# The second head mix of a talking-heads kernel, from two fp16 parts to float32 quarter tiles

## The chip, the core and the metric

One NeuronCore of a Trainium2 chip runs the whole program. Its engines run beside each other, each with its own instruction stream: TensorE (PE in the rows; PEld is its weight loads), VectorE (DVE), ScalarE (ACT), GpSimd (POOL) and SyncE (SP), which here issues the DMA transfers. The metric is the device time of one execution in microseconds (us), as the median over runs.

## The reference, cut to what matters

Talking-heads attention, then a gated MLP (only its attention part is touched by the change):

```
scores = q @ k^T / 8                          # 4 batches, 12 heads, 448 x 448, head size 64
scores = einsum('bhij,hg->bgij', scores, w_pre)    # first mix over the heads
p      = exp(scores - max over j);  p = p / (sum over j + 1e-9)
attn   = einsum('bhij,hg->bgij', p, w_post)        # second mix over the heads
x      = attn @ v                             # heads joined to 768 columns
out    = x + (gelu(x @ w_in)[u] * (w_sg @ layernorm(gelu(x @ w_in)[v]) + b_sg)) @ w_out
```

All data is float32 (w_in, w_out: float64).

## The kernel before

**Groups.** The rows of a score matrix (448 per batch) are cut into groups of 10 queries, 45 per batch and 180 in all. A group is a tile of 128 partitions: in each half of 64 stand 5 queries x 12 heads = 60 rows (and 4 that hold nothing), with the 448 keys along the free dimension. Such a tile makes both mixes a matmul over partitions: the first mix (`premix`, L962) contracts 60 rows with a block-diagonal w_pre, and so does the second (`postmix`, L1037) with w_post.

**A group's way** is the generator `slot` (L1080): row maximum on VectorE (L993), exp with its row sum on ScalarE (L1000, writes the float32 tile `p32`), the reciprocal of the sum, `rs` (L1005, L1006); then one of three preparations of the second mix, then `postmix` on TensorE, then `evict` (L1133), which copies the product from PSUM to `at16`, from where `av` (L1160, L1185) multiplies with v.

**The three preparations before.** Groups 9 to 44 are *full*: `w_norm` (L1008) multiplies a [128, 120] table of w_post by `rs`, and `postmix` runs four float32 matmuls on the whole 128x128 array (L1044: 112 key columns of p as stationary weights, 120 moving columns). All others make fp16 parts: either `p_hi_of` and `p_lo_of` (L1018, L1023: high part of p times rs, then the rest), or `p_norm`, `p_hi`, `p_lo` (L1028, L1013, L1032: normalise in place, high part, rest). Their `postmix` runs 24 fp16 matmuls as two row tiles of 64x128 (L1056: 3 products of parts x 4 key blocks x 2 halves, 60 moving columns). Two such groups, a pair, go through TensorE in one burst.

**TensorE's other work.** `qk_mm` (L842, L849) makes the scores of a pair of heads with 64x128 row tiles (chunks of 64 queries: 64x64 quarter tiles); `premix` uses 64x64 quarter tiles; `av` 128x64 column tiles; the MLP (`products`, L1210, L1217, and L1430) mostly the whole array. A tile mode is how the 128x128 array is divided; it changes whenever two neighbours in TensorE's order use different modes.

**The order** is set when the program is built: `Plan.run` (L294) takes the next step of each stream by due ranks and planned costs (pairs are due by their group number; steps that several engines can do go to the one that is planned to end first) and writes every engine's instructions in that order. An engine then runs its list strictly in order and waits where data is late. `mode_of` (L221) tells the planner the tile mode; a change of it costs a step C_MODE in the plan. Score parts go through DRAM (`s_d`): written by `write` (L872), fetched back as groups by `load_pair` (L939).

**Buffers.** `p32` has 3 buffers (N_P32), each freed when the fp16 parts are made (full groups: when `postmix` has run); the fp16 parts have rings of 4. The fp16 `postmix` of every pair uses the same two PSUM banks (`at2`), so it comes after the evictions of the pair ahead.

Of the kernel before, what the change touches and what calls it, by code (L numbers as in the profile page):

```python
# [10 lines left out]
F32 = mybir.dt.float32  # L11
F16 = mybir.dt.float16
# [3 lines left out]
ALU = mybir.AluOpType  # L16
# [20 lines left out]
N_P32 = 3  # L37
# [37 lines left out]
P_F32 = 0
P_ONE = (0, 1, .5, .5)
C_ONE = 1e9
D_ONE = 20
# [11 lines left out]
N_W = 0  # L90
# [9 lines left out]
def talking_heads_gmlp(ctx, tc, q, k, v, w_pre, w_post, w_in, g_ln, w_sg, b_sg, w_out, out):  # L100
    nc = tc.nc
# [51 lines left out]
    wpp = ctx.enter_context(tc.tile_pool(name="wpp", bufs=2))  # L153
# [30 lines left out]
    wpost = const.tile([P, H * NT], F32, name="wpost")  # L184
# [3 lines left out]
    wpc_hi = const.tile([P, H * NH], F16, name="wpc_hi")  # L188
    wpc_lo = const.tile([P, H * NH], F16, name="wpc_lo")
    p_ring = [[const.tile([P, (NC - 1) * TC + P], F16, name=f"p{w}{i}") for i in range(PR)] for w in "hl"]  # L190
# [8 lines left out]
    wpc32 = vn_hi.rearrange("p c f -> p (c f)")[:, 384:504].bitcast(F32)  # L199
# [21 lines left out]
    def mode_of(gen):  # L221

        name = gen.__name__
        if name == "slot":
            return "128x128" if gen.gi_frame.f_locals.get("full") else "64x128"
        if name == "all_parts":
            return "64x32"
        if name == "all_qk" and heads(gen.gi_frame.f_locals["i"]) == 4:
            return "64x64"
        return {"all_qk": "64x128", "all_premix": "64x64", "all_av": "128x64"}.get(name, "128x128")  # L230
# [782 lines left out]
    def p_hi(n):  # L1013
        x = st[n]
        x["ph"] = p_ring[0][n % PR][:, :S]
        cast(x["ph"], x["p32"])

    def p_hi_of(n):  # L1018
        x = st[n]
        x["ph"] = p_ring[0][n % PR][:, :S]  # L1020
        cast(x["ph"], x["p32"], x["rs"])

    def p_lo_of(n):  # L1023
        x = st[n]
        x["pl"] = p_ring[1][n % PR][:, :S]
        nc.vector.scalar_tensor_tensor(out=x["pl"], in0=x["p32"], scalar=x["rs"], in1=x["ph"], op0=ALU.mult, op1=ALU.subtract)  # L1026

    def p_norm(n):  # L1028
        x = st[n]
        cast(x["p32"], x["p32"], x["rs"])  # L1030

    def p_lo(n):  # L1032
        x = st[n]
        x["pl"] = p_ring[1][n % PR][:, :S]
        diff(x["pl"], x["p32"], x["ph"])

    def postmix(n):  # L1037
        x = st[n]
        w = H * NT
        if "wp" in x:  # L1040
            ps = x["at"] = at_banks(False)[n % 2]
            at["next"] = n + 1
            for jc in range(NC):
                nc.tensor.matmul(ps[:TC, jc * w:(jc + 1) * w], lhsT=x["p32"][:, jc * TC:(jc + 1) * TC], rhs=x["wp"], start=True, stop=True)  # L1044
            return

        hi, lo = (r[n % PR] for r in p_ring)
        at2 = at_banks(True)
        w = H * NH
        o = x["col"]  # L1050
        for jc in range(NC):
            js = slice(jc * TC, jc * TC + P)
            for k, (l, r) in enumerate(((hi, wpc_hi), (hi, wpc_lo), (lo, wpc_hi))):
                for hf in range(2):
                    rows = slice(64 * hf, 64 * hf + 64)
                    nc.tensor.matmul(at2[:, hf, o + jc * w:o + (jc + 1) * w], lhsT=l[rows, js], rhs=r[rows],  # L1056
                                     start=(k == 0), stop=(k == 2))

    def at_views(n):
# [18 lines left out]
    W_NORM = {"act": 330, "dve": 192, "pool": 486}, {"act": 197, "dve": 192}  # L1078

    def slot(n, t):  # L1080
        b, c, _ = glist[n]
        i = NCH * b + ORD.index(c)
        t = yield "dve", 552, n - 3, t
        softmax_max(n)
        t = yield "act", 645, n - 2.5, t, lambda: after([past("exp", n - 1), past("p32", n - N_P32)])
        softmax_exp(n)
        tm["exp", n] = t
        t = yield "dve", 278, n - 2, t, lambda: past("r", n - 1)
        norm_r(n)
        tm["r", n] = t  # L1090
        full = ND <= n < N_F32 and (n < N_FULL or n * P_F32 % 1 < P_F32 or ck["pe"] < max(ck["dve"], ck["pool"]) + C_F32)
        if full:
            t = yield None, W_NORM[n < N_W], n - 1, t, lambda: after([past("ph", n - 1), past("post", n - 2)])
            w_norm(n)
            tm["pn", n] = tm["ph", n] = tm["pl", n] = t
        elif n * P_ONE[b] % 1 < P_ONE[b] or n >= D_ONE and ck["dve"] + C_ONE < ck["pool"]:
            t = yield None, {"act": 560, "dve": Shared(363), "pool": 640}, n - 1.5, t, lambda: after([past("ph", n - 1), past("post", n - PR)])
            p_hi_of(n)
            tm["pn", n] = tm["ph", n] = t
            t = yield "dve", Shared(600), n - 1, t, lambda: past("pl", n - 1)  # L1100
            p_lo_of(n)
            tm["pl", n] = tm["p32", n] = t
        else:
            t = yield None, dict(ones(S), act=590, dve=Shared(363), pool=620), n - 1.9, t, lambda: past("pn", n - 1)
            p_norm(n)
            tm["pn", n] = t
            t = yield None, ones(S), n - 1.5, t, lambda: after([past("ph", n - 1), past("post", n - PR)])
            p_hi(n)
            tm["ph", n] = t
            t = yield None, twos(S), n - 1, t, lambda: past("pl", n - 1)  # L1110
            p_lo(n)
            tm["pl", n] = t
            tm["p32", n] = t
# [368 lines left out]
    with tc.manual_schedule():  # L1482
        nc.vector.memset(neg_half, -0.5)
        nc.vector.memset(wpre32, 0.0)
        for r in p_ring:
            for x in r:
                nc.gpsimd.memset(x[:, S:], 0.0)
# [97 lines left out]
        def mix_weights(e):  # L1585
# [9 lines left out]
            e.tensor_tensor(  # L1595
                out=wpost.rearrange("p (g t) -> p g t", t=NT),
                in0=wrep[:, 1, :].unsqueeze(2).to_broadcast([P, H, NT]),
                in1=msk[:, 0:2, :].rearrange("p a b -> p (a b)").unsqueeze(1).to_broadcast([P, H, NT]), op=ALU.mult)
# [4 lines left out]
            e.tensor_copy(out=wpc_hi, in_=wpc32)  # L1603
            e.tensor_tensor(out=wpc_lo, in0=wpc32, in1=wpc_hi, op=ALU.subtract)
# [100 lines left out]
```

## Time and profile before

| | |
|---|---|
| median of 3 runs | 581.94 us (581.2 to 585.87) |
| the profiled execution: first to last instruction | 579.8 us |
| busy: TensorE, weight loads | 562.8 us (97%), 370.8 us |
| busy: VectorE, ScalarE, GpSimd | 424.4, 416.1, 355.2 us |
| granted TensorE clock, mean | 0.994 |
| DMA | 112.69 MB, mean 194 GB/s |

The execution that was profiled has no time of its own beside its span of 579.8 us; the median of the runs lies 2.1 us above that span, which is what lies around it. Busy time of TensorE counts a matmul from its start to its modelled end, and neighbours overlap, so 97% says that it seldom stood still, not that it was at its peak. In a row such as `x48 | 0.77` the number behind x counts records; a float32 matmul is two records (and two weight loads).

### The profile page before, as it was taken

The numbers are of one execution on the slowest core, as the hardware profiler recorded it, in microseconds if no ns is written. First come the engines' busy times: TensorE is split into PE (matmuls) and PEld (weight loads), VectorE is DVE, ScalarE is ACT, GpSimd is POOL, SyncE is SP. The second block draws the span as 40 slices with busy tenths as digits, with TensorE's granted clock in tenths as the row PEclk, the third lists the DMA queues.
The fourth block names the chain that finished last, engine by engine and source line by source line (L and its number), as shares of the span: only waits on it lengthen the run. The fifth ranks groups of instructions, "written<-read, shape, count | busy, mean of one in ns | idle before, by whom it ended". The sixth has DMA issues, their size and how long they took to land.

```text
span 579.8 us, 22704 instructions
## 1 busy us (share of the span) xinstructions
PE 562.8 (97%) x9356; PEld 370.8 (64%) x9356; DVE 424.4 (73%) x1029; ACT 416.1 (72%) x968; POOL 355.2 (61%) x456
## 2 busy tenths in 40 slices
PE   8999999999999999999999988999999999999997
PEld 4554676667675746666666744768676757687754
DVE  5786687764889887669988876677889885566560
ACT  5688786787888677666879867777788697765221
POOL 6789574595766776535666797675755784654100
PEclk9999999999999999999999997999999999999999
DMA  9789998896698579889798876999795554510002
GB/s 223 193 251 252 278 293 244 248 252 192 193 257 240 175 206 255 198 201 200 207 260 248 231 227 179 190 264 219 199 243 162 178 189 131 161 35 2 2 1 95
DMA packets 98807, 112.69 MB, mean 194 GB/s; under 512 B 50596, under 2 KB 85932, under 8 KB 98704
## 3 DMA queue, kind: packets, MB, share of 16 engines
q1 hardware_dynamic: 98640, 111.24, 70.9%
q8 instruction: 73, 1.20, 0.9%
q14 instruction: 30, 0.25, 0.1%
q10 hardware_dynamic: 64, 0.00, 0.0%
HBM read 63.61 MB, written 42.10 MB: 182 GB/s over the span
## 4 chain that ended last, share of the span: by engine, by line
PE 74%; POOL 7%; DVE 6%; ACT 4%; DMA 4%; issue 3%; SPq 0%; POOLq 0%; ACTq 0%; DVEq 0%
PE ps_av L1185 12%; PE ps_x L1217 10%; PE ps_s L980 9%; PE ps_u L1217 9%; PE ps_v L1217 8%; PE at L1056 7%; PE ps_qk L849 6%; PE at L1044 5%; DMA kT<-st 2%; DMA st<-in_k_dram 1%; DVE nm L993 1%; ACT p L1000 1%; PE at L1217 1%; POOL pl L386 1%; PE ps_x L1430 1%
## 5 line engine op out<-in xcount | busy, mean ns | idle before, releaser
L1000 ACT ACTIVATE p<-ps_s,nm 128x448 f32<-128x448 f32 x180 | 114.2, 636 | 36.9 <-DVE nm L993 27.7
L993 DVE TENSOR_REDUCE nm<-ps_s 128x1 f32<-128x448 f32 x180 | 106.5, 617 | 33.8 <-PE ps_s L980 30.9
L381 ACT ACTIVATE at<-at 112x480 f32<-112x480 f32 x176 | 106.6, 619 | 28.1 <-PE at L1056 24.1
L381 ACT ACTIVATE s<-ps_qk 128x448 f16<-128x448 f32 (+3 forms) x140 | 70.2, 547 | 11.8 <-PE ps_qk L849 8.3
L1185 PE MATMUL ps_av<-at,v 112*64 112x120 f32 (+1 forms) x1536 | 77.9, 260 | 0.6 <-DVE s L869 0.6
L1185 PEld LDWEIGHTS ps_av<-at,v 112*64 112x64 f32 x1536 | 73.8, 137 | 5.8 <-issue 2.4
L1026 DVE SCALAR_TENSOR_TENSOR pl<-p,rs,ph 128x448 f16<-128x448 f32 x90 | 71.0, 788 | 4.4 <-POOL ph L383 2.5
L1056 PEld LDWEIGHTS <-ph 64*128 64x128 f16 x2304 | 53.1, 94 | 24.0 <-issue 15.0
L1217 PEld LDWEIGHTS <-wbuf 128*128 128x128 f16 x1152 | 58.3, 98 | 9.2 <-issue 6.6
L1217 PE MATMUL ps_u<-xTh,wbuf 128*128 128x128 f16 (+1 forms) x768 | 63.0, 213 | 0.3 <-DVE gbuf L1267 0.3
L849 PE MATMUL ps_qk<-kT,qT 64*128 64x448 f16 (+3 forms) x540 | 61.5, 358 | 1.1 <-DMA kT<-st 0.8
L386 POOL TENSOR_TENSOR pl<-p,ph 128x448 f16<-128x448 f32 x54 | 57.4, 1062 | 4.6 <-ACT ph L381 2.2
L383 POOL TENSOR_SCALAR ph<-p,rs 128x448 f16<-128x448 f32 x56 | 38.2, 683 | 34.8 <-DVE rs L1006 18.1
L1217 PE MATMUL ps_u<-xTl,wbuf 128*128 128x128 f16 (+1 forms) x384 | 59.2, 212 | 0.0
L1056 PE MATMUL at<-wpc_hi,ph 64*128 64x60 f16 x1152 | 58.3, 189 | 0.4 <-ACT at L381 0.4
L1056 PE MATMUL at<-wpc_lo,ph 64*128 64x60 f16 x1152 | 57.5, 188 | 0.0
L1056 PE MATMUL at<-wpc_hi,pl 64*128 64x60 f16 x1152 | 57.5, 188 | 0.0
L383 POOL TENSOR_SCALAR p<-p,rs 128x448 f32<-128x448 f32 x42 | 30.1, 716 | 44.8 <-DVE rs L1006 23.4
L1217 PE MATMUL ps_x<-wo,gbuf 128*128 128x384 f16 (+1 forms) x336 | 56.2, 332 | 0.5 <-POOL gbuf L386 0.5
L869 DVE SCALAR_TENSOR_TENSOR s<-ps_qk,s 128x448 f16<-128x448 f32 x84 | 49.3, 617 | 7.6 <-ACT s L381 6.7
L1005 DVE TENSOR_SCALAR rs<-ss 128x1 f32<-128x1 f32 x180 | 26.8, 149 | 34.0 <-ACT p L1000 32.6
L1056 PEld LDWEIGHTS <-pl 64*128 64x128 f16 x1152 | 49.5, 94 | 0.1
(236 smaller groups left out, 1222.3 us busy)
## 6 DMA issues: line engine op xcount, KB each, us to landing
g<-s_d SPq DMA_DIRECT2D x166, 210.0 KB
s_d<-s SPq DMA_DIRECT2D x18, 448.0 KB
s_d<-s SPq DMA_DIRECT2D x24, 280.0 KB
v<-in_v_dram SPq DMA_DIRECT2D x12, 448.0 KB
out_dram<-ot SPq DMA_DIRECT2D x24, 192.0 KB
s_d<-s SPq DMA_DIRECT2D x18, 252.0 KB
st<-in_k_dram SPq DMA_DIRECT2D x9, 448.0 KB
s_d<-s SPq DMA_DIRECT2D x18, 224.0 KB
```

Source lines behind the costliest of these rows:

```text
L381: e.activation(out=o, in_=i, func=AF.Copy, scale=scale)
L383: e.tensor_scalar(out=o, in0=i, scalar1=scale, scalar2=1.0, op0=ALU.mult, op1=ALU.mult)
L386: (e or pl.on).tensor_tensor(out=o, in0=a, in1=b, op=ALU.subtract)
L849: nc.tensor.matmul(ps[o * rows:(o + 1) * rows, :S], lhsT=qT2[i % 2][r, tq, h // 2 + o, :rows], rhs=kT[r, h // HG, tk, h // 2 % 2 + o, :], ...
L869: nc.vector.scalar_tensor_tensor(out=e[:, 1, :], in0=ps[:n, :S], scalar=1.0 / math.sqrt(D), in1=e[:, 0, :], op0=ALU.mult, op1=ALU.subtract)
L980: nc.tensor.matmul(st[m]["s2"][o:o + 64, :S], lhsT=w[rows], rhs=x[rows, u, :], start=(k == 0), stop=(k == len(terms) - 1))
L993: nc.vector.tensor_reduce(out=nm, in_=st[n]["s2"][:, :S], axis=AX.X, op=ALU.max, negate=True)
L1000: nc.scalar.activation(out=x["p32"], in_=x["s2"][:, :S], func=AF.Exp, bias=x["nm"], accum_out=x["ss"])
L1026: nc.vector.scalar_tensor_tensor(out=x["pl"], in0=x["p32"], scalar=x["rs"], in1=x["ph"], op0=ALU.mult, op1=ALU.subtract)
L1056: nc.tensor.matmul(at2[:, hf, o + jc * w:o + (jc + 1) * w], lhsT=l[rows, js], rhs=r[rows], start=(k == 0), stop=(k == 2))
L1185: nc.tensor.matmul(ps[a * D:(a + 1) * D, k3 * rows:(k3 + 1) * rows], lhsT=x[:, h, jc, :], rhs=y[:, jc, h, w:w + rows], start=(jc == 0 and ...
L1217: nc.tensor.matmul(o, lhsT=l, rhs=r, start=first, stop=last)
```

## The change

All 180 groups prepare the second mix in one way. `w_norm` multiplies a [128, 60] table of w_post (`wpc32`) by `rs`, and `postmix` runs float32 matmuls straight on `p32`, as 64x64 quarter tiles: 4 key blocks x 2 column tiles (64 and 48 key columns of p as weights) x 2 halves = 16 matmuls of 60 moving columns. No fp16 parts of p are made any more, and their rings are gone. All groups from 9 on go as pairs through the two banks `at2`. `p32` and `wp` have 6 buffers each and are freed by `postmix`. `qk_mm` now cuts its 128 output rows into two column tiles, so that all scores are 64x64 quarter tiles. The planner is told the new modes and costs and orders everything anew.

```diff
-N_P32 = 3
+N_P32 = 6
...
         if name == "slot":
-            return "128x128" if gen.gi_frame.f_locals.get("full") else "64x128"
+            return "64x64"
...
-        return {"all_qk": "64x128", "all_premix": "64x64", "all_av": "128x64"}.get(name, "128x128")
+        return {"all_qk": "64x64", "all_premix": "64x64", "all_av": "128x64"}.get(name, "128x128")
...
             for o in range(heads(i) // 2):
-                for a, ps in enumerate(pss):
-                    r = slice(a * D, (a + 1) * D)
-                    nc.tensor.matmul(ps[o * rows:(o + 1) * rows, :S], lhsT=qT2[i % 2][r, tq, h // 2 + o, :rows],
-                                     rhs=kT[r, h // HG, tk, h // 2 % 2 + o, :], start=(n == 0), stop=(n == 2))
+                for c in range(0, rows, 64):
+                    m = min(64, rows - c)
+                    for a, ps in enumerate(pss):
+                        r = slice(a * D, (a + 1) * D)
+                        nc.tensor.matmul(ps[o * rows + c:o * rows + c + m, :S], lhsT=qT2[i % 2][r, tq, h // 2 + o, c:c + m],
+                                         rhs=kT[r, h // HG, tk, h // 2 % 2 + o, :], start=(n == 0), stop=(n == 2))
...
     def w_norm(n):
         x = st[n]
-        x["wp"] = wpp.tile([P, H * NT], F32, tag="wp", name="wp")
-        cast(x["wp"], wpost, x["rs"])
...
+        x["wp"] = wpp.tile([P, H * NH], F32, tag="wp", name="wp")
+        cast(x["wp"], wpc32, x["rs"])
...
         for jc in range(NC):
-            js = slice(jc * TC, jc * TC + P)
-            for k, (l, r) in enumerate(((hi, wpc_hi), (hi, wpc_lo), (lo, wpc_hi))):
+            for j0, m in ((0, 64), (64, TC - 64)):
                 for hf in range(2):
                     rows = slice(64 * hf, 64 * hf + 64)
-                    nc.tensor.matmul(at2[:, hf, o + jc * w:o + (jc + 1) * w], lhsT=l[rows, js], rhs=r[rows],
-                                     start=(k == 0), stop=(k == 2))
+                    j = jc * TC + j0
+                    nc.tensor.matmul(at2[j0:j0 + m, hf, o + jc * w:o + (jc + 1) * w], lhsT=x["p32"][rows, j:j + m],
+                                     rhs=x["wp"][rows], start=True, stop=True)
...
-        t = yield "act", 645, n - 2.5, t, lambda: after([past("exp", n - 1), past("p32", n - N_P32)])
+        t = yield "act", 645, n - 2.5, t, lambda: after([past("exp", n - 1), past("post", n - N_P32)])
...
+        t = yield None, W_NORM, n - 1, t, lambda: after([past("wp", n - 1), past("post", n - N_P32)])
+        w_norm(n)
```

**What moves in the order.** First TensorE, in the stretch of the full groups (batch 0). The columns are line, operation, output<-inputs, output shape; `at` is the PSUM of the second mix, `ps_s` that of the first, `g` the scores fetched back. Before:

```order
L849 MATMUL ps_qk<-kT,qT_127 128x448
L1044 MATMUL at_1114<-wp,p_2008 112x120 x4
L980 MATMUL ps_s_2087<-g_121,wpre_98 64x448 x2
L1044 MATMUL at_1113<-wp,p_2055 112x120 x4
L675 LDWEIGHTS wo
```

And in that stretch after the change (L1112 is `av`, L967 `premix`, L1010 `postmix`):

```order
L1112 MATMUL ps_av<-at_119,v_118 64x120 x24
L967 MATMUL ps_s_2543<-g_113,wpre_98 64x448 x2
L967 MATMUL ps_s_2542<-g_113,wpre_98 64x448 x2
L1010 MATMUL at_453<-wp,p_2494 64x60 x2
L1010 MATMUL at_453<-wp,p_2494 48x60 x2
```

Before, every neighbour here is another tile mode, and a group stands by itself; after it, both groups of a pair follow (16 such rows) and behind them the scores of L836, which are 64x64 as well, so the mode does not change from the first mix to the scores.

Second, TensorE in the last batch. Before:

```order
L849 MATMUL ps_qk<-kT,qT_127 128x448
L1056 LDWEIGHTS ph_108
L1056 MATMUL at_2669<-wpc_hi,ph_108 128x60
L1056 LDWEIGHTS ph_108
L1056 MATMUL at_2669<-wpc_hi,ph_108 128x60
L1056 LDWEIGHTS ph_108
L1056 MATMUL at_2669<-wpc_lo,ph_108 128x60
```

After, where a pair follows an `av`:

```order
L1112 MATMUL ps_av<-at_119,v_118 64x120 x48
L967 MATMUL ps_s_4240<-g_113,wpre_98 64x448 x2
L967 MATMUL ps_s_4239<-g_113,wpre_98 64x448 x2
L1010 MATMUL at_453<-wp,p_4122 64x60 x2
L1010 MATMUL at_453<-wp,p_4122 48x60 x2
```

48 fp16 matmuls of a pair, each with its weight load, became 32 float32 ones. Counted over TensorE's whole order, the tile mode changes 386 times before and 278 times after; up to the 45th group it is 118 and 85.

Third, GpSimd near the end of batch 1, where the keys of the next batch (`st`) and the gating (`vs`, `gbuf`) are prepared. Before:

```order
L383 TENSOR_SCALAR st_7149<-st_7148 112x8x64 x2
L383 TENSOR_SCALAR ph_110<-p_7239 128x448
L386 TENSOR_TENSOR st_7149<-st_7148,st_7149 112x8x64 x2
L1390 TENSOR_TENSOR vs<-vs,gbuf 128x448
L386 TENSOR_TENSOR pl_114<-p_7239,ph_110 128x448
L383 TENSOR_SCALAR p_7355<-p_7355,rs 128x448
```

After, at one such place (L368, L371 and L1317 are the helpers of L383, L386 and L1390):

```order
L368 TENSOR_SCALAR wp<-wpc_101,rs 128x60
L368 TENSOR_SCALAR st_4206<-st_4205 112x8x64 x2
L368 TENSOR_SCALAR wp<-wpc_101,rs 128x60
L371 TENSOR_TENSOR st_4206<-st_4205,st_4206 112x8x64 x2
L1317 TENSOR_TENSOR vs<-vs,gbuf 128x448 x2
L371 TENSOR_TENSOR gbuf<-vs,gbuf 128x448 x2
L368 TENSOR_SCALAR wp<-wpc_101,rs 128x60 x2
```

The steps on whole p tiles are gone from GpSimd's queue; a small `wp` per group stands in it instead, between the same long steps. Of the 180, GpSimd gets 144, ScalarE 35 and VectorE 1.

## Rows read from the trace of the kernel before

**Rows 1.** The page: busy time, busy tenths in 40 slices, granted clock, DMA

```profile
PE 562.8 (97%) x9356; PEld 370.8 (64%) x9356; DVE 424.4 (73%) x1029; ACT 416.1 (72%) x968; POOL 355.2 (61%) x456
...
PEclk9999999999999999999999997999999999999999
DMA  9789998896698579889798876999795554510002
```

**Rows 2.** The page: chain of waits that ended last, share by engine

```profile
PE 74%; POOL 7%; DVE 6%; ACT 4%; DMA 4%; issue 3%; SPq 0%; POOLq 0%; ACTq 0%; DVEq 0%
```

**Rows 3.** The chain in order of time: start us, length us, what

```profile
74.97 1.00 PE at L1044 x8
...
76.35 0.82 PE at L1044 x8
...
255.79 0.77 PE at L1056 x48
```

**Rows 4.** Timeline of PE: start us, length us, what, rows*columns of the tile

```profile
344.08 0.22 PE L1430 MATMUL ps_x<-ident_x,xTh 128*128 128x128 f16 x1
344.14 0.22 PE L1430 MATMUL ps_x<-ident_x,xTl 128*128 128x128 f16 x1
344.29 0.36 PE L849 MATMUL ps_qk<-kT,qT 64*128 64x448 f16 x2
```

**Rows 5.** Timeline of weight loads, same columns

```profile
113.40 0.30 PEld L1304 LDWEIGHTS ps_v<-mv,diff 128*128 128x128 f32 x2
...
114.40 0.21 PEld L980 LDWEIGHTS ps_s<-g,wpre 60*64 60x64 f32 x8 [0.37 <-issue]
```

**Rows 6.** Timeline of PE: bursts in column tiles, quarter tiles and row tiles

```profile
111.68 0.76 PE L849 MATMUL ps_qk<-kT,qT 64*64 64x448 f16 x12
...
113.73 0.74 PE L849 MATMUL ps_qk<-kT,qT 64*128 64x448 f16 x6
114.40 0.98 PE L980 MATMUL ps_s<-g,wpre 60*64 60x448 f32 x8
...
509.81 5.14 PE L1185 MATMUL ps_av<-at,v 112*64 112x120 f32 x96
514.88 0.57 PE L980 MATMUL ps_s<-g,wpre_hi 60*64 60x448 f16 x8
```

**Rows 7.** Windows: length, busy PE, PEld, DVE, ACT, POOL, clock, DMA share, GB/s

```profile
54.00:150.00 96.00, 93.79 (x1043) 66.42 (x1045) 65.91 (x179) 75.16 (x187) 62.83 (x77) 1.00 0.85 245
150.00:532.00 382.00, 374.75 (x7290) 247.42 (x7288) 299.65 (x732) 288.76 (x672) 247.68 (x302) 0.99 0.75 198
```

**Rows 8.** Windows of 20 us, same columns

```profile
300.00:320.00 20.00, 20.00 (x406) 12.77 (x404) 17.52 (x44) 17.94 (x44) 13.55 (x18) 1.00 0.94 242
340.00:360.00 20.00, 15.70 (x217) 8.24 (x218) 14.52 (x29) 12.52 (x30) 15.77 (x18) 0.83 0.63 187
380.00:400.00 20.00, 20.00 (x413) 14.69 (x411) 14.39 (x39) 13.58 (x33) 11.04 (x13) 1.00 0.99 259
```

**Rows 9.** Timeline of POOL, ACT and PE around the longest stop

```profile
343.21 2.27 POOL L386 TENSOR_TENSOR st<-st,st 112x512 f16<-112x512 f32 x2
...
345.43 1.53 POOL L1390 TENSOR_TENSOR vs<-vs,gbuf 128x448 f32<-128x448 f32 x1
...
346.93 1.02 POOL L386 TENSOR_TENSOR pl<-p,ph 128x448 f16<-128x448 f32 x1
347.98 0.63 ACT L1000 ACTIVATE p<-ps_s,nm 128x448 f32<-128x448 f32 x1 [1.94 <-POOL pl L386]
...
348.76 0.85 PE L980 MATMUL ps_s<-g,wpre_hi 60*64 60x448 f16 x6 [2.34 <-ACT p L1000]
```

**Rows 10.** Groups of instructions: busy us, mean ns; idle before, releaser

```profile
L1026 DVE SCALAR_TENSOR_TENSOR pl<-p,rs,ph 128x448 f16<-128x448 f32 x90 | 71.0, 788 | 4.4 <-POOL ph L383 2.5
...
L386 POOL TENSOR_TENSOR pl<-p,ph 128x448 f16<-128x448 f32 x54 | 57.4, 1062 | 4.6 <-ACT ph L381 2.2
...
L383 POOL TENSOR_SCALAR wp<-wpost,rs 128x120 f32<-128x120 f32 x29 | 13.5, 464 | 23.9 <-DVE rs L1006 17.8 <-PE ps_ws L675 3.8 <-ACT qT L381 0.9
```

More of the change, by code (lines that the diff above doesn't have):

```diff
@@ L68 @@
 C_TR = 110
-N_F32 = 45
-N_FULL = 45
-C_F32 = -2000
 N_AV = 4
-PR = 4
 B_DT = 2
[L75 to L78, printed above, removed]
 L_CL = 750
@@ L89 @@
 K_PART = 8.6
-N_W = 0
 K_D1 = 2
@@ L152, in talking_heads_gmlp @@
     p32p = ctx.enter_context(tc.tile_pool(name="p32p", bufs=N_P32))
-    wpp = ctx.enter_context(tc.tile_pool(name="wpp", bufs=2))
+    wpp = ctx.enter_context(tc.tile_pool(name="wpp", bufs=N_P32))
     dram = ctx.enter_context(tc.tile_pool(name="dram", bufs=1, space=DRAM))
@@ L183, in talking_heads_gmlp @@
     msk = const.tile([P, 2, NH], F32, name="msk")
-    wpost = const.tile([P, H * NT], F32, name="wpost")
+    wpc32 = const.tile([P, H * NH], F32, name="wpc32")
     gln = const.tile([P, KC], F32, name="gln")
@@ L187, in talking_heads_gmlp @@
     warm = const.tile([P, 1], F32, name="warm")
-    wpc_hi = const.tile([P, H * NH], F16, name="wpc_hi")
-    wpc_lo = const.tile([P, H * NH], F16, name="wpc_lo")
-    p_ring = [[const.tile([P, (NC - 1) * TC + P], F16, name=f"p{w}{i}") for i in range(PR)] for w in "hl"]
     neg_half = const.tile([P, 1], F32, name="neg_half")
@@ L198, in talking_heads_gmlp @@
     vn_hi = const.tile([P, NM, DH], F16, name="vn_hi")
-    wpc32 = vn_hi.rearrange("p c f -> p (c f)")[:, 384:504].bitcast(F32)
     mskc_t = vn_hi.rearrange("p c f -> p (c f)")[:, 504:520].bitcast(F32)
@@ L224, in mode_of @@
         if name == "slot":
-            return "128x128" if gen.gi_frame.f_locals.get("full") else "64x128"
+            return "64x64"
         if name == "all_parts":
             return "64x32"
-        if name == "all_qk" and heads(gen.gi_frame.f_locals["i"]) == 4:
-            return "64x64"
-        return {"all_qk": "64x128", "all_premix": "64x64", "all_av": "128x64"}.get(name, "128x128")
+        return {"all_qk": "64x64", "all_premix": "64x64", "all_av": "128x64"}.get(name, "128x128")
     class Shared(float):
@@ L1009, in w_norm @@
         x = st[n]
-        x["wp"] = wpp.tile([P, H * NT], F32, tag="wp", name="wp")
-        cast(x["wp"], wpost, x["rs"])
[L1013 to L1035, printed above, removed]
+        x["wp"] = wpp.tile([P, H * NH], F32, tag="wp", name="wp")
+        cast(x["wp"], wpc32, x["rs"])
     def postmix(n):
         x = st[n]
[L1039 to L1047, printed above, removed]
         at2 = at_banks(True)
@@ L1062, in at_views @@
         outs = [x[:, :, :, a:a + NT] for x in (at_hi, at_lo, at32)]
-        if "at" in st[n]:
-            src = st[n]["at"][:TC, :NC * H * NT].rearrange("p (a t) -> p a t", t=NT)
-            return (src, *(o.rearrange("p c h t -> p (c h) t") for o in outs))
         o = st[n]["col"]
@@ L1076, in postmix_lo @@
         nc.vector.tensor_tensor(out=lo, in0=src, in1=hi, op=ALU.subtract)
-    W_NORM = {"act": 330, "dve": 192, "pool": 486}, {"act": 197, "dve": 192}
+    W_NORM = {"act": 250, "dve": 150, "pool": 380}
     def slot(n, t):
@@ L1090, in slot @@
         tm["r", n] = t
[L1091 to L1113, printed above, removed]
+        t = yield None, W_NORM, n - 1, t, lambda: after([past("wp", n - 1), past("post", n - N_P32)])
+        w_norm(n)
+        tm["wp", n] = t
         st[n]["col"] = 0
-        pair = not full and n >= ND and pair_of[n] == pair_of[n - 1]
-        if not full and n >= ND and n + 1 < NG and pair_of[n] == pair_of[n + 1]:
-            tm["p", n] = t
+        pair = n > ND and pair_of[n] == pair_of[n - 1]
+        if n >= ND and n + 1 < NG and pair_of[n] == pair_of[n + 1]:
             return
@@ L1121, in slot @@
         both = [n - 1, n] if pair else [n]
-        t = yield "pe", 1000 if full else 310 * len(both), n, t, lambda: after(
-            [past("post", both[0] - 1), past("lo", both[0] - (2 if full and n > ND else 1))])
+        t = yield "pe", 440 * len(both), n, t, lambda: after([past("post", both[0] - 1), past("lo", both[0] - 1)])
         for m in both:
@@ L1126, in slot @@
             tm["post", m] = t
-        if full:
-            tm["p32", n] = t
         if pair:
@@ L1484, in talking_heads_gmlp @@
         nc.vector.memset(wpre32, 0.0)
-        for r in p_ring:
-            for x in r:
-                nc.gpsimd.memset(x[:, S:], 0.0)
         wu = v_hi.rearrange("p h c d -> p (h c d)")[:, :512]
@@ L1594, in mix_weights @@
             e.tensor_scalar(out=wrep[:, 1, :], in0=wrep[:, 1, :], scalar1=S_WPOST, scalar2=None, op0=ALU.mult)
[L1595 to L1598, printed above, removed]
             wpc = wpc32.rearrange("p (g t) -> p g t", t=NH)
@@ L1602, in mix_weights @@
                 in1=mskc.unsqueeze(1).to_broadcast([P, H, NH]), op=ALU.mult)
-            e.tensor_copy(out=wpc_hi, in_=wpc32)
-            e.tensor_tensor(out=wpc_lo, in0=wpc32, in1=wpc_hi, op=ALU.subtract)
         for a in range(2):
```

## The prediction

> **What bounds the kernel now.** First the page: TensorE is busy 562.8 of 579.8 us, the other engines 61 to 73%, the granted clock is full (2.4 GHz) in all slices but one, and DMA is dense until the last sixth [rows 1]. The chain of waits lies on TensorE for 74% of the span; what is left is spread thin over the others [rows 2]. So the time is TensorE's work plus the 17 us in which it stands still (579.8 - 562.8) [rows 1]. Then the cost of a burst, in the chain in order of time. A full group that follows work in its own tile mode takes 0.82 us; one that has to change the mode takes 1.00 us [rows 3]. A fp16 pair takes 0.77 us, with one change of mode in it [rows 3]. The price of that change stands in the timeline: neighbours of 128 columns start 0.06 us apart, and the first matmul of another mode starts 0.15 us after the last [rows 4], so the array is empty for about 0.094 us. Last the windows, since the change gives in one stretch and takes in another: 54 to 150 us holds the full groups, 150 to 532 us the rest of the attention [rows 7].
>
> **The second mix, before.** Full: 36 x 0.82 = 29.5 us, and for the 28 of them that come behind another mode 0.09 us each for the first weight load (1.00 - 0.82 - 0.094), 2.5 us; together 32.0 us. fp16: (0.77 - 0.094) / 2 = 0.338 us a group [rows 3], x 144 = 48.7 us. Sum 80.7 us, changes of mode left out.
>
> **The second mix, after.** No row shows float32 quarter tiles with so few moving columns. A group has 16 matmuls, each of two records (weight load and matmul), on four tiles: 8 rounds of four. Two things can set a round. The streaming: the AV burst puts 96 records of 120 columns, two tiles at a time, into 5.07 us (to the start of the next burst, 0.094 of it the change) [rows 6], 0.104 us a pair of records, so 60 columns take about 0.052 us. The weight load: where the matmul has almost no columns, the second load of 128 float32 columns ends 0.30 us after the first began [rows 5]; with some 0.19 us for one alone that is 0.11 us a load, 0.055 us for 64 columns. Are the four loads made side by side? In the first mix eight loads of 64 float32 columns, two for each tile, end 0.21 us after the first began [rows 5]; one after the other they would need 8 x 0.055 = 0.44 us. And does a load hide under streaming? In AV it does: 0.104 us a round, not 0.052 x 2 + 0.055. So a round is the larger of the two, 0.055 us: 0.44 us a group, 79.2 us for 180, and 0.055 us for the first load of the 29 bursts that follow another mode: 80.8 us. Ends: 0.052 us (75.1 us in all) and 0.062 us, a load with some start of its own (91 us).
>
> So the second mix costs TensorE what it did, but in other places: groups 9 to 44 save 32.0 - 36 x 0.44 - 0.3 = 15.9 us; the other 144 pay 0.102 us each, 14.7 us, and the first loads 1.3 us.
>
> **Changes of mode.** The instruction order has 386 before and 278 after: 108 x 0.094 = 10.2 us saved, 33 of them (3.1 us) up to group 45 and 75 (7.1 us) behind it.
>
> **Scores as quarter tiles.** A burst with 64x64 tiles lasts 0.76 us for 12 matmuls, one with 64x128 tiles 0.74 us for 6 [rows 6]: the same work at the same price. The smaller loads hide under 448 columns. Nothing, but it is what lets three kinds of work stand in one mode.
>
> **Work off TensorE.** The parts go: VectorE loses 71.0 us, GpSimd 57.4 us of `pl` and the `ph` and p steps beside it; instead each group has a `wp` of half the width that cost GpSimd 0.464 us [rows 10]. None of these engines is the bound, so this pays only where TensorE waited for them. The place is 340 to 360 us: TensorE is busy 15.7 of 20 us there and the clock falls to 1.2 GHz for a while (mean 0.83) [rows 8]. The rows read: GpSimd works through two key steps and one gating step, only then makes a `pl`; exp waited 1.94 us for that `pl`, since one of three `p32` buffers hangs on it; the first mix waited 2.34 us for exp, and the clock fell behind that stop [rows 9]. Six buffers, freed by TensorE, take this wait away: up to 4.3 us of standing and 3.4 us of work lost to the clock (0.17 x 20). I take 6. What is late next is `wp`: it stands in the same queue of GpSimd behind the same key and gating steps (2.27, 1.53 us each [rows 9]), and TensorE waits for it in order; all that TensorE holds behind that pair waits with it. I put 1 us against the 6, and keep -7.7 and +3 as ends.
>
> **How much of the early gain arrives.** TensorE gets 19 us (15.9 + 3.1) less to do in a stretch of 96 us in which no other engine is relieved: full groups had no parts. ScalarE has 75.2 us there and the DMA engines 0.85 x 96 = 81.6 us [rows 7]. Elsewhere ScalarE reaches 17.94 of 20 us with TensorE never idle, and DMA 0.99 [rows 8], so a full TensorE bears 0.90 and 0.97; the stretch can't go below 75.2 / 0.9 = 84 us, or 81.6 / 0.97 = 84 us. That leaves 12 of the 19. Ends: 5 and 19.
>
> **The sum.** 579.8 - 12 (full groups) + 16.0 - 7.1 (the rest: mix and modes) - 5 (waits) = 571.7 us of span. The nine groups before 54 us are in the +16. With the 2.1 us by which the median of the runs lies above the span: **573.8 us**, -1.4%. The prologue and the MLP tail from 532 us on are unchanged.
>
> **Rivals.**
> *The early stretch does not shrink.* For it: 0.85 of DMA and 75.2 us of ScalarE in 96 us already, with transfers queued one behind the other; only 5 us arrive, and TensorE stands where it worked. The rest pays in full, waits give 2: 579.8 - 5 + 8.9 - 2 + 2.1 = 583.8 us, no change. Against it: DMA carried 0.94 to 0.99 for whole windows while TensorE was never idle [rows 8].
> *All of it arrives.* 19 instead of 12, and the waits give 7: 579.8 - 19 + 8.9 - 7 + 2.1 = 565 us.
> *Four quarter tiles don't work side by side (slower).* If a load could not run while its neighbour in the same rows streams, a round is 0.055 + 0.052 = 0.107 us, a group 0.86 us, the second mix 154 us instead of 80.8: 573.8 + 73 = 647 us. It decides from a round of 0.061 us on: then the mix costs 89 us, and the 8.1 us of the forecast are gone. Against it speak the AV rows, whose two column tiles share their rows and still hide their loads [rows 6], and the eight loads in 0.21 us [rows 5]; for it, that no row shows four tiles reloaded round after round: the first mix's burst of 0.98 us [rows 6] ends after two rounds.
> On this the Trainium skill (TensorE: Matmul & The Clock Gate, Part 3, what overlaps) says that a weight load overlaps matmuls in flight only if it goes to another row group. By that rule this rival would be the forecast, 647 us; the AV rows of this trace disagree with it.
> The skill's TensorEngine Tiling (Array Packing), Instruction Overhead, also warns not to take a tiling factor out of a dimension that is already small, since a matmul has a fixed cost of about 60 cycles. By that the 60 columns would gain nothing from four tiles; the trace holds 48 matmuls of 60 columns in 0.676 us [rows 3], 0.014 us each, below 60 cycles of a 2.4 GHz clock, so side by side that floor does not add up here.
>
> **Chances.** Forecast (567 to 580) 0.52; all arrives 0.16; no shrink 0.22; slower by serial tiles 0.10. Runs of this kernel spread by 0.8%, so about 1% (5.8 us) is what can be told from no change. Faster by over 1% (below 576.1 us): 0.37 of the first, 0.16 of the second, 0.01 of the third = 0.54. Within 1%: 0.15 + 0.19 = 0.34. Slower: 0.02 + 0.10 = 0.12. The range leaves out the last rival and the far ends: 564 to 586 us.
>
> **What would show it.** Right: bursts of `postmix` pairs of 0.88 to 0.98 us; the 45th group some 12 us earlier; the second mix at 79 to 83 us of TensorE; no wait of exp for a buffer; a full clock through batch 2. Wrong: a round far from 0.055 us (then the mix was mis-sized); pauses of TensorE between 50 and 140 us before the first mix (early gain lost); waits of `postmix` for `wp` behind key or gating steps of GpSimd.

## The result, and the profile after

The changed kernel takes **590.4 us** (median of 4 runs, 586.6 to 593.0), the kernel before beside it 581.7 us (581.2 to 585.9): ratio 1.013, 95% interval 1.009 to 1.016. It is 1.3% slower; forecast were 573.8 us and a range up to 586. The profiled execution took 593.0 us, the longest of the four, of which the span is 591.3 us: 11.5 us more than the profiled span before (the medians differ by 8.7 us).

The page of the changed kernel first: busy time with the number of instructions, granted clock, DMA share, and the queue that brings instructions (packets, MB, share of the DMA engines).

```profile
PE 560.1 (95%) x11804; PEld 391.6 (66%) x11804; DVE 370.1 (63%) x950; ACT 386.2 (65%) x922; POOL 234.7 (40%) x372
...
PEclk9999999999999999999999899999999999999999
DMA  9869898999596688798799678899785644600002
...
q8 instruction: 92, 1.51, 1.1%
```

Against [rows 1] all other engines have less to do, as intended, and TensorE is busy for 2.7 us less although the span grew by 11.5 us: it stands still for 31 us instead of 17. The column to look at is the count: 11,804 matmuls and as many weight loads, 26% more than before. They came in 92 packets of the instruction queue (the page before: 73 packets, 1.20 MB), so a packet of 16 KB holds some 257 TensorE instructions.

What TensorE waited for in the changed kernel (us in total, times, longest):

```profile
PE ps_v L1144 <- issue: 3.2, 3, 1.2
PE ps_qk L836 <- issue: 2.8, 2, 1.5
PE at L1010 <- issue: 2.2, 3, 1.3
PE ps_u L1144 <- issue: 2.1, 1, 2.1
PE ps_qk L836 <- DMA qT<-st: 1.9, 2, 1.3
PE ps_av L1112 <- issue: 1.7, 1, 1.7
PE at L1010 <- ACT at L366: 1.5, 2, 1.2
PE ps_qk L836 <- ACT s L366: 1.4, 2, 1.3
```

"issue" is time in which it waited for nothing that the profile shows. Here it leads the list with 12.0 us in 10 stops; the kernel before has no such row. Real waits for data hardly changed: 14.8 us against 13.2. Such a stop looks like this in TensorE's timeline (start, length, what):

```profile
325.01 0.28 PE L1144 MATMUL ps_u<-xTh,wbuf 128*128 128x128 f16 x2
325.12 0.22 PE L1144 MATMUL ps_u<-xTl,wbuf 128*128 128x128 f16 x1
327.46 0.29 PE L1144 MATMUL ps_u<-xTh,wbuf 128*128 128x128 f16 x2 [2.12 <-issue]
327.58 0.22 PE L1144 MATMUL ps_u<-xTl,wbuf 128*128 128x128 f16 x1
```

It lies in the middle of an MLP burst that the change doesn't touch, between two matmuls of the same tiles. Two things mark all ten stops in the trace's records. Each ends 1.3 to 1.6 us after a packet of the instruction queue has landed (such a packet is 1.15 us on its DMA engine). And counting TensorE's instructions from the start (the first is number 0), each stands ahead of an instruction whose number leaves 193 when divided by 256: a place in the instruction stream, not in the program. This stop, the longest, costs more than itself; behind the other nine the granted clock stays full. Windows behind it (length, busy PE, PEld, DVE, ACT, POOL, clock, DMA, GB/s) show the granted clock at 1.2 GHz for a while:

```profile
327.40:329.40 2.00, 1.94 (x30) 1.95 (x31) 0.11 (x1) 0.00 (x0) 2.00 (x4) 0.85 0.49 127
329.40:331.40 2.00, 2.00 (x24) 1.42 (x24) 0.00 (x0) 0.00 (x0) 1.15 (x2) 0.50 1.00 313
331.40:333.40 2.00, 2.00 (x34) 1.26 (x27) 1.20 (x3) 0.62 (x2) 0.00 (x0) 0.79 0.80 244
```

**Where the 11.5 us are.** In the table each matmul's streaming time (columns and passes at 2.4 GHz) is laid out from its start; a gap of up to 0.093 us at a change of mode counts as the change, gaps over 0.04 us beyond that as standing. How short gaps are sorted moves single entries by up to 7 us and the differences between columns by up to 2 us. The columns are the two long stretches, from group 9 to 45 and from 45 to 180; "without stops" is the first experiment below.

| us of TensorE | 9-45 before | after | without stops | 45-180 before | after | without stops |
|---|---|---|---|---|---|---|
| second mix | 29.5 | 16.9 | 17.4 | 46.5 | 62.9 | 64.9 |
| changes of mode | 7.7 | 5.0 | 5.0 | 23.9 | 18.2 | 18.1 |
| other work | 52.3 | 61.6 | 61.8 | 296.1 | 290.5 | 288.4 |
| waits for data | 3.4 | 9.7 | 9.5 | 9.2 | 2.8 | 1.9 |
| stops without a wait | 0 | 2.8 | 0 | 0.2 | 11.1 | 0 |
| small gaps | 3.0 | 1.1 | 1.3 | 3.4 | 3.0 | 1.8 |
| stretch | 95.8 | 97.2 | 95.1 | 379.3 | 388.4 | 375.0 |

Ahead of group 9 and behind group 180 the changed kernel takes 53.3 and 52.4 us, before 53.8 and 50.9. These are the rows of the changed kernel that answer to [rows 6] and [rows 7, 8], bursts and then windows:

```profile
254.08 1.09 PE L1010 MATMUL at<-wp,p 64*64 64x60 f32 x64
255.10 0.50 PE L1144 MATMUL ps_x<-wo,gbuf 128*128 128x384 f16 x2
```

```profile
54.00:150.00 96.00, 86.03 (x2006) 60.61 (x2006) 67.33 (x177) 75.53 (x188) 56.64 (x75) 1.00 0.90 252
150.00:540.00 390.00, 378.52 (x8617) 271.54 (x8608) 246.15 (x652) 261.44 (x632) 149.65 (x241) 1.00 0.74 193
...
340.00:360.00 20.00, 19.94 (x441) 12.15 (x442) 14.27 (x38) 13.28 (x34) 14.22 (x19) 1.00 0.81 191
```

The pair's burst lasts 1.02 us to the next start, 0.93 without the change of mode: 0.058 us a round. 340 to 360 us is full, as forecast. 54 to 150 us is emptier: 86 us of 96 instead of 94.

### The profile page after: what moved, and what is told of

Read it like the earlier page. It is cut to its first block, busy times and chain, and to the rows that moved or that the text cites. A ratio compares the mean times of both kernels' runs of the same rounds, so it can differ in the third digit from the quotient of the medians.

```text
span 591.3 us, 27431 instructions
## 1 busy us (share of the span) xinstructions
PE 560.1 (95%) x11804; PEld 391.6 (66%) x11804; DVE 370.1 (63%) x950; ACT 386.2 (65%) x922; POOL 234.7 (40%) x372
## 4 chain that ended last, share of the span: by engine, by line
PE 74%; DMA 2%; issue 2%; ACT 1%; DVE 1%; POOL 0%; SPq 0%; ACTq 0%; POOLq 0%; DVEq 0%
PE ps_x L1144 13%; PE at L1010 12%; PE ps_av L1112 11%; PE ps_u L1144 10%; PE ps_v L1144 9%; PE ps_s L967 9%; PE ps_qk L836 6%; DMA qT<-st 2%; PE ps_x L1357 2%; PE at L1144 1%; PE ps_ws L660 1%; ACT p L987 0%; POOL gbuf L587 0%; PE ps_q L384 0%; DVE nm L980 0%
## 5 line engine op out<-in xcount | busy, mean ns | idle before, releaser
L368 POOL TENSOR_SCALAR wp<-wpc,rs 128x60 f32<-128x60 f32 x144 | 47.8, 332 | 217.5 <-DVE rs L993 172.0
L1010 PEld LDWEIGHTS at<-wp,p 64*64 64x64 f32 (+1 forms) x5760 | 99.6, 127 | 25.8 <-issue 14.3
L1010 PE MATMUL at<-wp,p 64*64 64x60 f32 (+1 forms) x5760 | 105.2, 217 | 4.9 <-issue 2.2
L1112 PE MATMUL ps_av<-at,v 112*64 112x120 f32 (+1 forms) x1536 | 78.2, 260 | 1.8 <-issue 1.7
L1112 PEld LDWEIGHTS ps_av<-at,v 112*64 112x64 f32 x1536 | 74.0, 137 | 5.9 <-issue 2.6
L836 PE MATMUL ps_qk<-kT,qT 64*64 64x448 f16 (+1 forms) x972 | 64.9, 353 | 7.4 <-issue 2.8
L836 PEld LDWEIGHTS <-qT 64*64 64x64 f16 (+1 forms) x972 | 30.4, 106 | 27.4 <-issue 15.4
L967 PE MATMUL ps_s<-g,wpre 60*64 60x448 f32 x324 | 46.0, 554 | 1.3 <-ACT p L987 0.6
L1144 PEld LDWEIGHTS <-gbuf 128*128 128x128 f16 (+1 forms) x384 | 30.9, 101 | 19.5 <-issue 3.6
L987 ACT ACTIVATION_READ_ACCUMULATOR p<-ps_s,nm 128x1 f32 x180 | 37.4, 208 | 0.0
L366 ACT ACTIVATE xTh<-ps_av 128x360 f16<-128x360 f32 (+1 forms) x32 | 14.5, 452 | 33.4 <-PE ps_av L1112 33.3
L1144 PE MATMUL ps_v<-wv_lo,xTh 128*128 128x512 f16 (+1 forms) x120 | 34.4, 337 | 2.0 <-issue 2.0
```

The costliest lines, as they stand in the source:

```text
L836: nc.tensor.matmul(ps[o * rows + c:o * rows + c + m, :S], lhsT=qT2[i % 2][r, tq, h // 2 + o, c:c + m], rhs=kT[r, h // HG, tk, h // 2 % 2 + ...
L967: nc.tensor.matmul(st[m]["s2"][o:o + 64, :S], lhsT=w[rows], rhs=x[rows, u, :], start=(k == 0), stop=(k == len(terms) - 1))
L987: nc.scalar.activation(out=x["p32"], in_=x["s2"][:, :S], func=AF.Exp, bias=x["nm"], accum_out=x["ss"])
L1010: nc.tensor.matmul(at2[j0:j0 + m, hf, o + jc * w:o + (jc + 1) * w], lhsT=x["p32"][rows, j:j + m], rhs=x["wp"][rows], start=True, stop=True)
L1112: nc.tensor.matmul(ps[a * D:(a + 1) * D, k3 * rows:(k3 + 1) * rows], lhsT=x[:, h, jc, :], rhs=y[:, jc, h, w:w + rows], start=(jc == 0 and ...
L1144: nc.tensor.matmul(o, lhsT=l, rhs=r, start=first, stop=last)
```

## The experiments

Theory F: TensorE runs out of fetched instructions. Rival O: the new order of the work, and waits that come with it, cost the time. "Stops" are the "issue" rows of TensorE's waits, "waits" all its other rows.

**Half the records, same order (e1).**

```
-   matmul(at2[j0:j0+m, hf, o+jc*w : o+(jc+1)*w], lhsT=p32[rows, j:j+m],     rhs=wp[rows])            # float32
+   matmul(at2[j0:j0+m, hf, jc%2*200 : +280],     lhsT=ident[rows, j0:j0+m], rhs=wp[rows, 0:40] x 7)  # fp16
```

> The changed kernel with the same order on every engine, but each matmul of the second mix is a fp16 one of 280 columns (weights from a constant, moving data from wp, read seven times) in place of a float32 one of 60: by the columns a round of four tiles takes the same time (280 columns against the 0.058 us for a half of it), with half the records: about 5,800 of TensorE's 23,600 instructions fewer. What it computes in the second mix is not the reference. Theory F (TensorE runs out of fetched instructions: in the changed kernel eleven stops of 0.2 to 2.3 us, 13.9 us together, lie in the middle of bursts, wait for nothing, and each ends 1.3 to 1.6 us after a 16 KB packet of the instruction queue has landed): the stops vanish, 574 to 579 us. Rival O (the new order of bursts and its waits cost the time): nothing changes, 588 to 593 us. If TensorE's own work were the cause, 588 to 593 us as well, with the stops gone and standing for data in their place.

Measured: **576.7 us**, 0.989 of before (0.982 to 0.996). Page and windows, columns as above:

```profile
PE 558.1 (97%) x8924; PEld 373.6 (65%) x8924; DVE 368.9 (64%) x950; ACT 385.5 (67%) x922; POOL 234.5 (41%) x372
...
54.00:150.00 96.00, 88.77 (x1499) 59.90 (x1495) 67.18 (x177) 78.75 (x195) 57.13 (x75) 1.00 0.92 253
150.00:522.00 372.00, 370.83 (x6344) 253.65 (x6340) 243.49 (x650) 256.39 (x622) 148.14 (x240) 1.00 0.77 201
```

No stop is left, and waits are 12.2 us. The bursts of the second mix cost as much as in the changed kernel (table), every queue has the same order, and 13.7 us are gone. Rival O falls: what the new order costs is in this run too. e1 also takes float32 and the reading of p out of the mix; e11 below has the stops in fp16, and e5 has them where no data is waited for.

**The supply by itself (e5).** A kernel with nothing but bursts of the second mix, 40 pairs three times over.

```
for n in range(40): quarter(0); quarter(240)              # no loads yet
for n in range(384): sync.dma_start(ring[n % 16], q[...]) # 256-byte packets, from here on
for n in range(40): quarter(0); quarter(240)
for n in range(40): quarter_half(0); quarter_half(240)    # the form of e1
```

> The disputed cost by itself: TensorE alone works through 40 pairs of the changed second mix back to back (128 instructions a pair) with no transfers, then 40 pairs beside a steady stream of loads of 256-byte packets, then 40 pairs in the form with half the records and the same columns, beside what is left of the loads. Output: zeros. A pair needs 0.93 us by its rounds, so 37 us a stage. Theory F: in the changed kernel a packet of 256 instructions takes 1.15 us and is taken up 1.3 us later, while such pairs use up 256 instructions in 1.86 us: stage one stops every 256 instructions even without transfers (50 to 80 us), stage two stops longer (60 to 120 us), stage three least (37 to 45 us). Rival (the stops come from something else in the full kernel, a hidden wait or a port): each stage 37 to 40 us.

Timeline of TensorE in stage one, and windows of the three stages (length, busy PE, PEld, DVE, POOL, clock, DMA, GB/s):

```profile
31.13 2.09 PE L48 MATMUL at<-wp,p 64*64 64x60 f32 x128 [1.64 <-issue]
34.86 2.09 PE L48 MATMUL at<-wp,p 64*64 64x60 f32 x128 [1.64 <-issue]
38.59 2.09 PE L48 MATMUL at<-wp,p 64*64 64x60 f32 x128 [1.64 <-issue]
42.31 2.09 PE L48 MATMUL at<-wp,p 64*64 64x60 f32 x128 [1.64 <-issue]
```

```profile
13.00:85.40 72.40, 43.88 (x2398) 40.98 (x2396) 1.25 (x16) 0.00 (x0) 0.93 0.14 47
85.40:168.50 83.10, 51.85 (x2595) 48.68 (x2596) 0.00 (x0) 0.00 (x0) 0.86 0.77 171
168.50:210.00 41.50, 39.05 (x1245) 36.84 (x1244) 0.00 (x0) 0.00 (x0) 1.00 0.79 177
```

This is the effect with nothing else in the way (one run; the output of zeros is written until some 23 us, behind that stage one has no transfers but the instruction packets): 128 matmuls and their 128 loads run, then TensorE stands, every 3.73 us, again ahead of number 193 of 256. A pair needs 0.93 us by its rounds. The first window holds 37.5 pairs (2,398 records of 64 a pair), which need 35 us and take 72 us; the second holds 40 pairs beside the loads, 37 us by the rounds, and takes 83 us. In the third 39 pairs in the form with half the records take 41.5 us. Theory F's numbers hold in all three; the rival's 37 to 40 us don't.

**The cost put into the kernel before (e11).** Same order, fp16 parts, twice the records.

```
-   for hf in range(2): matmul(at2[:, hf, ...], lhsT=l[rows, js], rhs=r[rows])
+   for j0, m in ((0, 64), (64, 48)):
+       for hf in range(2): matmul(at2[j0:j0+m, hf, ...], lhsT=l[rows, j:j+m], rhs=r[rows])
```

> The suspected cost put into the kernel before: its fp16 second mix as quarter tiles (twice the matmuls, half the columns of weights each), order kept on every engine, 6,900 TensorE instructions more (25,700, more than the changed kernel has). Theory F: stops in the middle of bursts that wait for nothing, 15 to 40 us together, where the kernel before has none; what a burst costs beside them is open between 0.6 us (by its columns, four tiles at a time) and 1.35 us (0.014 us a record, as in every dense burst so far) in place of 0.77: 585 to 660 us. Rival (stops need float32 or the new order): no stops, 570 to 625 us.

Measured: 621.4 us, 1.070 (1.066 to 1.074). Its leading waits:

```profile
PE at L1057 <- issue: 17.2, 14, 3.3
PE ps_s L980 <- ACT p L1000: 3.8, 3, 1.9
PE ps_av L1186 <- issue: 2.9, 3, 1.0
PE ps_u L1218 <- issue: 1.9, 2, 1.5
```

With the rows left out here 22.4 us of stops in 20, all ahead of number 193; waits are 11.6 us. Neither float32 nor the new order is needed for them. A pair's burst without a stop takes 0.82 us from first to last start (median; 0.65 in the kernel before), within the bounds left open.

**Another seed for the changed kernel (e4), and for the one before (e6).** `SEED = 10` becomes 11 in each.

> The changed kernel with another seed of the planner's jitter: another order of the same work, nothing else (a control for what a new order alone moves). Theory F: the bursts are as dense, so stops in the middle of bursts again, ten or so of them at other places, 10 to 16 us together, 586 to 594 us. Rival O: the order decides, so the time may fall to 578 us without the stops going away or rise by as much.

> The kernel before with another seed of the planner's jitter and nothing else: what a new order alone does to it. If a plan scatters by 1% or more, part of the 16 us of the run with quarter tiles of scores alone is the new plan: 584 to 596 us. If plans are alike, 580 to 584 us, and quarter tiles of scores cost 14 us in some way that their bursts don't show.

e4: 591.2 us, 1.014 (1.008 to 1.020); 10.9 us in eight stops at other times, all again ahead of number 193. e6: 583.7 us, 1.003 (0.998 to 1.007). So the slowdown is no accident of one order. e6 has 0.9 us of stops in two: the kernel before stood close to the edge already.

**Scores undone (e2), alone (e3), alone in the old order (e9).** e2 puts the 64x128 matmul back into the changed kernel; e3 and e9 put the loop over halves into the kernel before, and e3 also tells the planner of the new mode:

```
    matmul(ps[o*rows : (o+1)*rows], lhsT=qT2[.., :rows], rhs=kT)                        # e2
    for c in range(0, rows, 64): matmul(ps[o*rows+c : +m], lhsT=qT2[.., c:c+m], ..)     # e3, e9
    return {"all_qk": "64x64", ...}                                                     # e3, in mode_of
```

> The changed kernel with one part undone: scores as 64x128 tiles again, planned anew. 864 TensorE instructions fewer (22,700), some 67 changes of mode more. Theory F: still dense bursts of the second mix (128 instructions in 0.93 us), so most of the stops stay; 2 us less of scores, 6.3 us more of mode changes (67 x 0.094), a few us less of stops: 588 to 594 us. Rival O (a plan in which scores, first mix and second mix share one mode puts TensorE ahead of its data): standing falls, 580 to 585 us.

> The kernel before with one part of the change alone: scores as 64x64 quarter tiles, planned anew; as many mode changes as before (380 against 376), 864 instructions more on TensorE (19,600 against 18,700). Prediction on record: quarter tiles cost nothing, 582 us. By the trace of the changed kernel their bursts cost 2 us: 584 us. Theory F adds a stop or two at most: 584 to 587 us. Rival O has no number for it but the scatter of a new plan.

> The kernel before with scores as 64x64 quarter tiles and its own order on every engine kept (the planner is not told of the new mode): the price of the quarter tiles without a new plan. 864 TensorE instructions more, 8 changes of mode more. By the bursts of the changed kernel: 1 to 2 us of scores, 0.8 us of modes, one or two stops of the instruction supply: 583 to 587 us. Rival (the 16 us of the replanned run belong to the quarter tiles themselves): 594 to 600 us.

e2: 588.9 us, 1.010 (1.006 to 1.013), as expected in time but not in kind. Stops fell from 12.0 to 2.1 us with only 4% fewer instructions, so they do not follow the total (the last section counts what they follow); 59 more changes of mode in the trace (5.4 us) and some 4 us of second mix and keep-warm matmuls gave most of it back. e3: 598.7 us, 1.028 (1.021 to 1.034), above all that was expected. e9 tells why: with the old order the quarter tiles cost **3.0 us** (1.006, 1.003 to 1.009), 2.3 of them in two stops. The rest of e3 is its new plan. Their leading rows, e3 and then e9:

```profile
PE ps_s L980 <- ACT p L1000: 5.5, 5, 1.9
PE ps_q L397 <- DMA q<-in_q_dram: 2.7, 1, 2.7
PE ps_v L1303 <- DVE mv L1299: 2.0, 1, 2.0
```

```profile
PE ps_s L982 <- ACT p L1002: 3.5, 3, 1.9
PE at L1058 <- issue: 2.3, 2, 1.8
```

e3 waits 19.6 us for data, e9 10.4. e6 had moved by only 0.3% on a new order, so a re-plan can cost from nothing to 2%; one plan of each says no more.

**Smaller lumps (e7).** The second mix group by group: `both = [n]` for `both = [n - 1, n] if pair else [n]`.

> The changed kernel with the second mix burst by burst for one group (64 instructions in 0.46 us) in place of a pair (128 in 0.93), planned anew. The same instructions in all, in smaller lumps. Theory F: what counts is how many instructions TensorE takes between two landings of the instruction queue (several us apart), so lumps of half the size help only in part: stops of 6 to 13 us instead of 13.5, 580 to 592 us. Rival (only the back-to-back pairs drain the supply): stops below 3 us, 576 to 580 us.

Measured: 598.9 us, 1.025 (1.018 to 1.031), a miss in the time. Stops are 8.2 us, less than 12.0 and within the bounds, but TensorE now waits for the eviction of each group, the first row here, and its tile mode changes 66 times more than in the changed kernel, some 6 us at 0.094 us each:

```profile
PE at L1010 <- ACT at L366: 7.0, 13, 1.1
PE at L1010 <- issue: 6.4, 5, 2.2
PE at L1010 <- POOL wp L368: 1.9, 2, 1.0
```

**How much of an early saving arrives (e8, e12).** The kernel before, same order, full groups made light; e12 takes the wait for `wp` out as well.

```
-   matmul(ps[:TC, ...], lhsT=p32[:, jc*TC : (jc+1)*TC], rhs=wp)          # float32
+   matmul(ps[:TC, ...], lhsT=ident[:, :TC],             rhs=wp)          # e8: fp16
+   matmul(ps[:TC, ...], lhsT=ident[:, :TC],             rhs=ident[:, :w]) # e12
```

> The kernel before, same order on every engine, with the second mix of the 36 full groups as four fp16 matmuls of 120 columns (weights from a constant) in place of float32 ones: 0.82 us becomes about 0.2 us, so TensorE has some 22 us less to do up to group 45, with no more instructions. The second mix of these groups is not the reference's. It asks how much of an early saving arrives. Theory on record: the stretch is bounded by ScalarE and the transfers at about 12 us of gain: group 45 at 137 to 139 us instead of 149.6, and the end 10 to 12 us earlier, 570 to 572 us. Rival (the early stretch hardly shrinks, as in the changed kernel without its stops, where group 45 came 2.8 us earlier): group 45 at 143 to 148 us, 574 to 580 us.

> The run with light full groups once more (kernel before, same order, four fp16 matmuls of 120 columns for the second mix of groups 9 to 44), now with moving data from a constant too: TensorE waits neither for wp nor for exp there; wp is still made, nobody reads it. The second mix of these groups is not the reference's. In the run before TensorE waited 6.4 us for wp out of GpSimd's queue, and group 45 came at 143.6 us. Theory on record (floor of 84 us for the stretch from ScalarE and the transfers): without that wait group 45 comes at 137 to 140 us, the end 570 to 574 us. Rival (the 6.4 us are only the last of several waits that lie side by side: the data of the next step is late as well): group 45 at 141.5 to 144 us, others waited for instead, 575 to 578 us.

e8: 577.9 us, 0.991 (0.987 to 0.994); group 45 at 143.6 us. e12: 576.4 us, 0.993 (0.989 to 0.997); group 45 at 142.2. The rivals had it both times: of 22 us taken off TensorE 6 and 7 arrive at group 45 (149.6 us before). TensorE's waits between 50 and 150 us, of e8 and then of e12:

```profile
PE at L1044 <- POOL wp L383: 6.4, 5, 2.2
PE ps_k L399 <- DVE xTl L1195: 1.6, 2, 1.4
PE ps_qk L849 <- ACT s L381: 1.4, 3, 0.6
```

```profile
PE ps_k L399 <- DVE xTl L1195: 2.7, 2, 1.8
PE ps_qk L849 <- ACT s L381: 1.6, 3, 0.8
PE ps_v L1217 <- DVE s L383: 1.4, 1, 1.4
PE at L1044 <- ACT at L381: 1.3, 2, 1.0
```

With the longest wait gone many short ones for several engines take its place: by these rows no single queue bounds the stretch.

**A version to beat both (e10).** Float32 quarter tiles for groups 9 to 44 alone, the rest as before.

```
    if "wp" in x:
-       matmul(ps[:TC, jc*w : (jc+1)*w], lhsT=p32[:, jc*TC : (jc+1)*TC], rhs=wp)
+       (the 16 quarter-tile matmuls of the change, columns 0 or 240 in turn)
```

> A version that might beat both: the kernel before with the change's second mix (float32 quarter tiles) for the full groups 9 to 44 alone, fp16 parts and scores as before for the rest, planned anew. TensorE loses 36 x 0.36 = 13 us of the early work, 1,700 instructions more (20,500). Theory F: with the supply loaded little, few stops (2 to 5 us); of an early saving of 22 us 6 arrived at group 45 and 4 at the end, so of 13 about 3: 578 to 584 us. Rival (all of an early saving arrives once the groups are light in wp too): 570 to 574 us.

Measured: 586.9 us, 1.011 (1.006 to 1.015), slower than either expected. Stops are 0.4 us, as theory F has it, but waits rise to 22.4 us in 37: of some 9 us less work and modes less than nothing arrives. No version that computes the whole reference was found that beats the kernel before.

## Why the prediction was wrong

**The step that failed is the sum itself: it priced TensorE by what the array does, and had no term for handing it the instructions.** It counted 16 matmuls of two records each, eight rounds of four, and asked only how long a round takes. By the same count a pair is 128 instructions in 0.93 us, 138 a microsecond; e5 shows the supply at 256 in 3.73 us, 69 a microsecond, and in 4.1 us beside transfers. Over the whole run TensorE asks for only 40 a microsecond (23,608 in 591 us), so it is short only where dense bursts meet a late packet: ten times here, 12.0 us by the waits and 13.9 by the table, more than the whole loss. Without the stops (e1) the same order takes 576.7 us, 3 us from the forecast. That nearness hides errors that cancel: up to group 45 it gains 2.7 us (12 forecast), and from there to group 180 it gains 4.2 us where a loss of 3.9 (16.0 - 7.1 - 5) was forecast, since some 7 us of work had moved forward.

Point by point. *Second mix*: before 79.0 us in the trace (80.7 forecast), after 84.1 (80.8). The round came at 0.058 us, within the bounds of 0.052 and 0.062: a term mis-sized by 3 us, and 5.1 us more than before instead of 0.1. (The lower end of that term, 75.1 us, comes to 74.9 by its own 0.052 us, 76.4 with the first loads; nothing hangs on it.) *Four quarter tiles side by side*: right, and the 647 us rival with its serial tiles is out; 16 rounds in 0.93 us leave no room for it. The rule of the Trainium skill that would have given it (TensorE: Matmul & The Clock Gate, Part 3) does not hold for these bursts. *Changes of mode*: 387 to 291 in the trace, 8.7 us saved (10.2 forecast). *Scores as quarter tiles*: not free; 2.0 us of bursts in the changed kernel, 3.0 us in e9. *Waits*: the stop at 346 us is gone as described, though the clock still fell once, at 329 us behind the longest stop without a wait; past group 45 waits fell by 6.4 us (5 forecast); `wp` behind GpSimd's queue came to 1.1 us (1 set against it). *Early gain*: too high. The 45th group was to come 12 us earlier; it comes at 150.5 us (149.6 before), in e1 at 146.9. Mix and modes gave 15.3 us between groups 9 and 45 (19 forecast), in e1 14.8. In e1 9.5 us were filled with other work moved forward, some 7 of them first mix and MLP that are missing later, and 6.1 with new waits for data: with the 0.7 us by which the stretch is shorter some 7.6 us arrive, not 12. The floor of 84 us, from ScalarE's and the transfers' busy time, was reached in no run; with most of TensorE's mix gone (e12) the stretch still takes 88.7 us.

The rival that ended slower had the wrong mechanism. The right one could have been suspected ahead, though the kernel before has no such stop: its page shows 73 packets of instructions for 18,712, and the text multiplied records by durations without setting their rate against that queue.

## What to carry over

Cutting a matmul into more tiles buys array time with instructions: count loads and matmuls as well, and set the rate of the densest burst against what the instruction queue has been seen to bring. A pause of TensorE in the middle of a burst, put down to "issue", ahead of the same number modulo 256 each time and ending 1.2 to 1.7 us after an instruction packet has landed, is this; look for it in bursts that the change did not touch. A saving on the busiest engine of a stretch in which ScalarE and the transfers are busy for 80 to 90% too should not be priced in full: here a quarter (e8), a third (e12), a half (e1) and less than nothing (e10) of it arrived.

## What was not expected of the hardware

TensorE alone, with no transfers, gets 256 instructions per 3.73 us in e5; beside 171 GB/s of transfers per 4.1 us. In all fourteen traces every gap of over 0.9 us between two TensorE instructions for which nothing was waited for stands ahead of number 193 of 256, and so do all ten stops of the changed kernel, the short ones too. In the changed kernel packet j (the first is 0) begins on its DMA engine 1.0 to 6.3 us (median 2.8) after TensorE's instruction 256 j + 128 has begun; what sets that delay, and whether recording a trace adds to it, was not tried.

The same records tell when a stop comes. A stop that ends behind packet j stands ahead of number 256 j + 449, which is 321 instructions behind 256 j + 128. From the start of the latter to 1.35 us after packet j has landed it takes 3.4 to 8.8 us in the changed kernel, 3.5 to 8.8 in the one before: the packets came no later. But TensorE works through such 321 instructions (a stop taken out) in 4.0 us at the least after the change, 5.5 before. It needs under 6 us for them 3 times in the kernel before (no stop), 21 in the changed one (10 stops), 13 in e2 (4), never in e1 (none) and 44 in e11 (20). So a stop is a fast stretch that meets a late packet. e2 lost stops with its fast stretches; why it lost more of them than of the stretches stays open.

Records can run closer than in any row before: 96 fp16 quarter-tile matmuls of 60 columns start within 0.82 us in e11 (median), 0.009 us each.
